# Stacking two of the four batches the other way round, so that the 64x64 score products address all four quadrants of TensorE

## The chip, the core and the metric

The kernel runs on one core of one Trainium2 chip. The metric is the device time of one execution in microseconds (us), and less is better. Three executions of the kernel before took 624.39 to 625.46 us, with a median of 624.98 us.

## The reference

Two layers follow each other, in float32. The first is a linear recurrence over time (RWKV time mixing) for 4 batches, 8 heads, 768 tokens and 48 channels per head:

```python
for t in range(S):
    cur = einsum('bhd,bhe->bhde', u[None] * k[t], v[t])
    y[t] = einsum('bhd,bhde->bhe', r[t], state + cur)
    state = w[None, :, :, None] * state + einsum('bhd,bhe->bhde', k[t], v[t])
```

Its output, 3072 tokens of 384 features, goes into a gated feed-forward network with a root-mean-square norm ahead of it:

```python
xn = x / sqrt(mean(x * x, axis=-1) + 1e-06) * rms_g
g = xn @ w_gate
out = (g * sigmoid(g) * (xn @ w_val)) @ w_out      # 384 -> 1536 -> 384
```

## The kernel before

**Time mixing in chunks.** The 768 tokens are cut into 12 chunks of 64 (`NS`, `L`). Within a chunk the recurrence becomes matrix products: scores between the chunk's keys and receptances, weighted by powers of the decay `w`, times the values, plus the state from before the chunk. `mixing(s)` adds the operations of chunk `s` to a plan. The names of its steps, which the text uses, are these:

- R: `decay_r` multiplies r by the decay powers `up`, on DVE, into the tile `ME`. Rc: `copy_r` copies the odd heads' partitions 64 to 127 into `MO`, on ACT. K: `decay_k` multiplies k by `down` in place, on DVE.
- A: `products` forms the scores on TensorE. Of the 8 heads, the even ones lie on partitions 0 to 47 and the odd ones on partitions 64 to 111 (side `z`). There are 4 batches, 4 pairs of heads and 2 sides, so 32 products of 48x64 by 48x64. Even heads use rows 0 to 63 of the array and write PSUM partitions 64 to 127; odd heads use rows 64 to 127 and write partitions 0 to 63. Two batches (one `half`) fill one bank (`at`), and the two halves are done one after the other.
- d: `diagonal` puts the bonus for the current token on the diagonal of the scores' tile, on ACT, from `du`, which DVE computes with three passes over `TOK` (`bonus_1` to `bonus_3`, the second with the table `utab`). m: `masked` copies the scores below the diagonal over it, on DVE.
- Y: `outputs` multiplies `ME` and `MO` (half scores, half decayed r) with `VS` (half values, half state), 32 products of 128x64 by 128x64 on TensorE. The two sides write different halves of the PSUM partitions.
- h and U: `state_k` weights the keys with the table `wk`, and `states` forms the new state, on TensorE. `keep_states` copies it back.
- After Y, `keep_squares`, `keep_outputs` and a norm (`scaled` on DVE) give `xa`, and `exchange` copies it with its partition halves swapped into `xb`.

Chunk 0 (`quick`, `early`) is done differently: A goes half by half, the diagonal comes from an extra product E of `ku`, and the weighted keys come from a product T (`turn_k`).

**Feed-forward.** Chunks 0 and 1 go through plain gate, value and output products (`gate_val`, `add_cell`), while the weights arrive from memory in pieces. Each piece is loaded by SP, split by ACT (`ulp`) and DVE (`bits`) and joined by GpSimd (POOL). Later chunks are taken two at a time through a seven-product scheme (`group`, `second_layer`). A product of this kind is 6 matmuls of 64x128 by 64x256.

**What sets the order.** `Plan.add` takes each operation with its engine, an assumed cost, and the names that it reads and writes. `Plan.schedule` lays them out by assumed start times and due times. `Plan.search` tries 4 times 2000 random changes of those due times for the operations of the first chunks. `Plan.give` then issues everything in the order of the planned starts. So each engine's order is fixed when the kernel is built, and waits between engines are semaphores. The plan prices A at 2.0 us. `warm` fills idle stretches of TensorE in the first 27 us of the plan with products of `ones`. One of these is two records in the trace.

**How the trace shows a matmul.** Every float32 matmul of the program stands in the trace as two LDWEIGHTS and two MATMUL records. The 32 products of one A are therefore 64 MATMUL records.

Of the kernel before, what the change touches and what calls it, by code (L numbers as in the profile page):

```python
# [41 lines left out]
FP32 = mybir.dt.float32  # L42
# [8 lines left out]
P = 128  # L51
# [10 lines left out]
B, H, S, D = 4, 8, 768, 48  # L62
HP = H // 2
L = 64
# [175 lines left out]
def fast(ctx, tc, chan, tok, vpad, wka, wkb, wot, cols, u_row, out, bad):  # L240
# [23 lines left out]
    def c_tile(shape, name, dtype=FP32):  # L264
        return const.tile(shape, dtype, name=name)
# [4 lines left out]
    wraw, ucol, gcol = col[:, 0:HP], col[:, HP : 2 * HP], col[:, 2 * HP :]  # L270
    utab = c_tile([P, HP, D], "utab")
    eps = c_tile([P, 1], "eps")
# [17 lines left out]

    ident = c_tile([P, P], "ident")
    make_identity(nc, ident)
# [24 lines left out]
    gdup = rows_out[:, 0].rearrange("p j f -> p (j f)")[:, 0 : HP * 2 * L].rearrange("p (h z t) -> p h z t", h=HP, z=2)  # L317
    wk = c_tile([P, HP, D], "wk")
    pows = {1: wcol}
# [18 lines left out]
    def keep_token_powers(bank):  # L338
        ps = bank.rearrange("p (h c) -> p h c", h=HP)
        act.copy(wk[64:128], ps[64:128, :, 0:D])  # L340
        act.copy(wk[0:64], ps[0:64, :, 64 : 64 + D])

    def state_decay(z, p):

        rows = slice(64 * z, 64 * z + D)
        act.mul(
            KH[rows, z, :, p, :], free_dims(ident[rows, 64 * z : 64 * z + D], (0, B), (1, D)), pows[L][rows, p : p + 1]
        )

    def w_range():  # L350
# [20 lines left out]
    def load_u():  # L371
        for z in range(2):
            src = bass.AP(tensor=u_row.tensor, offset=u_row.offset + z * HP * D, ap=[[0, 64], [1, HP * D]])
            sp.dma_start(out=utab[64 - 64 * z : 128 - 64 * z].rearrange("p h d -> p (h d)"), in_=src)

# [53 lines left out]

    def decay_r(s, lo=0, hi=B):  # L430

        dve.tensor_mul(ME[:, lo:hi], CH[:, 0, lo:hi], free_dims(up, (0, hi - lo), (L, HP), (1, L)))

    def copy_r(s, lo=0, hi=B):
        act.copy(MO[64:128, lo:hi], ME[64:128, lo:hi])

    def decay_k(s, lo=0, hi=B):
        dve.tensor_mul(CH[:, 1, lo:hi], CH[:, 1, lo:hi], free_dims(down, (0, hi - lo), (L, HP), (1, L)))

    def bonus_1(s):  # L440
        dve.tensor_mul(TOK[:, 0], TOK[:, 0], TOK[:, 1])

    def bonus_2(s):
        dve.tensor_mul(TOK[:, 0], TOK[:, 0], free_dims(utab, (0, B), (D, HP), (1, D)))

# [26 lines left out]
    def state_k(s, z):  # L472

        rows = slice(64 - 64 * z, 128 - 64 * z)
        dve.tensor_mul(KH[rows, z], TOK[rows, 1], free_dims(wk[rows], (0, B), (D, HP), (1, D)))

    def turn_k(bank, half):

        pk = bank[:, 0 : 2 * HP * D].rearrange("p (b h d) -> p b h d", b=2, h=HP)
        for bl in range(2):  # L480
            b = 2 * half + bl
            for p in range(HP):
                for z in range(2):
                    rows = slice(64 * z, 64 * z + D)
                    pe.matmul(
                        pk[64 - 64 * z : 128 - 64 * z, bl, p, :], CH[rows, 1, b, p, :], KH[rows, z, b, p, :], start=True,
                        stop=True, skip_group_check=True,
                    )
# [5 lines left out]

    def products(bank, half, ks, even, odd):

        pa = bank.rearrange("p (b h t) -> p b h t", b=2, h=HP)
        for bl in range(2):
            b = 2 * half + bl
            for p in range(HP):  # L500
                for rows, to, m in ((slice(0, D), slice(64, 128), even), (slice(64, 64 + D), slice(0, 64), odd)):
                    pe.matmul(
                        pa[to, bl, p, :], ks[rows, b, p, :], m[rows, b, p, :], start=True, stop=True,
                        skip_group_check=True,
                    )

# [9 lines left out]
    def outputs(bank, half):  # L516

        py = bank.rearrange("p (i t) -> p i t", i=HP)
        for bl in range(2):
            b = 2 * half + bl  # L520
            for p in range(HP):
                for z, m in ((0, ME), (1, MO)):
                    pe.matmul(
                        py[64 * z : 64 * z + 64, p, bl * L : (bl + 1) * L], VS[:, z, b, p * L : (p + 1) * L],
                        m[:, b, p, :], start=True, stop=True, skip_group_check=True,
                    )
# [219 lines left out]
    def mixing(s):  # L746
# [3 lines left out]
        if early:  # L750
            t = "ac"[s]
            add("ACT", 1.6, ["w", "CHk0", "CHk1"], ["ku"], lambda: u_k(s, ku), name=f"ku {s}")
            for half in range(2):
                add(
                    "PE", 1.05, ["ku", "CHr0", "CHr1"], [f"{t}{half}"],
                    lambda half=half: products(bank_of[t][:, half], half, ku, CH[:, 0], CH[:, 0]), name=f"E {s}",
                    rows=True,
                )
        else:
            add("DVE", 0.95, ["TOKk"], ["TOKr"], lambda: bonus_1(s), port=True, name=f"bonus1 {s}")  # L760
            add("DVE", 0.95, ["utab"], ["TOKr"], lambda: bonus_2(s), port=True, name=f"bonus2 {s}")
            add("DVE", 0.94, ["TOKr"], ["du"], lambda: bonus_3(s), name=f"bonus3 {s}")
        for part in ((0, 2), (2, 4)) if early else ((0, 4),):
            hs = range(part[0] // 2, part[1] // 2)
            n = len(hs)
            keys = lambda *names: [f"{x}{h}" for x in names for h in hs]
            add(
                "DVE", 0.12 + 0.55 * n, ["up"] + keys("CHr"), keys("MEr", "MEt"),
                lambda part=part: decay_r(s, *part), port=True, name=f"R {s}",
            )  # L770
            add("ACT", 0.16 + 0.44 * n, keys("MEt"), keys("MOr"), lambda part=part: copy_r(s, *part), name=f"Rc {s}")
            add(
                "DVE", 0.12 + 0.55 * n, ["down"], keys("CHk"), lambda part=part: decay_k(s, *part), port=True,
                name=f"K {s}",
            )
        two = [next_at() for _ in range(2)]

        def scores(half):
            products(two[half][0], half, CH[:, 1], ME, MO)

        score_keys = [[f"CHk{half}", f"MEr{half}", f"MOr{half}"] for half in range(2)]
        if quick:
            for half in range(2):
                add("PE", 1.05, score_keys[half], [two[half][1]], lambda half=half: scores(half), name=f"A {s}", rows=True)
        else:
            add(
                "PE", 2.0, score_keys[0] + score_keys[1], [two[0][1], two[1][1]], lambda: [scores(0), scores(1)],
                name=f"A {s}", rows=True,
            )
# [82 lines left out]
        else:  # L872
# [11 lines left out]
            else:  # L884
# [8 lines left out]
                add("DVE", 0.35, ["ms'"], ["ms"], lambda: refine(ms[:, 0], ms[:, 1]), name=f"inv {s}")  # L893
            add("DVE", 0.4, ["ms"], ["diag"], lambda: on_diagonal(ms[:, 0], diag), port=True, name=f"diag {s}")
            add("PE", 0.45, ["diag"], [key], lambda bank=bank: spread(bank, diag), name=f"spread {s}")
# [5 lines left out]
        if not turned:  # L901
# [3 lines left out]
        add(  # L905
            "PE", 1.58, ["KH0", "KH1", "VSv", "VSs0", "VSs1"] + [f"khd{z}{i}" for z in range(2) for i in range(HP)],
            [last[0][1], last[1][1]], lambda: [states(last[half][0], half) for half in range(2)], name=f"U {s}",
# [9 lines left out]
    add("DVE", 0.43, ["pw"], ["down"], lambda: dve.tensor_mul(down, pw_rev, by_inv), port=True, name="down")  # L917
    add("DVE", 0.22, [], ["dmask"], lambda: dve.tensor_add(dmask, ident[:, 0:64], ident[:, 64:128]), port=True)
    for z in range(2):
        for i in range(HP):  # L920
            add("ACT", 0.34, ["pw"], [f"khd{z}{i}"], lambda z=z, i=i: state_decay(z, i), name="khd")

    def token_tables():
        add(
            "DVE", 0.86, ["pw"], ["r0", "r1"], lambda: [
                dve.tensor_mul(gdup[:, :, z, :], pw_rev, free_dims(pows[L // 2], (1, HP), (0, L))) for z in range(2)
            ], port=True, name="gdup",
        )
        bank, key = next_at()
        add("PE", 0.9, ["r0", "r1"], [key], lambda bank=bank: token_powers(bank), name="wk")  # L930
        add("ACT", 0.7, [key], ["wk"], lambda bank=bank: keep_token_powers(bank), name="wk")

# [76 lines left out]
    add("DVE", 0.4, ["w"], ["count"], w_range)  # L1009
    add("DVE", 0.0, ["rounded", "up", "down", "wk", "dmask", "ku"], ["sums"], begin_sums)  # L1010
    for n, reads, writes in (
# [679 lines left out]
```

## Time and profile before

| what | value |
|---|---|
| median of three executions | 624.98 us (624.39 to 625.46) |
| profiled execution: span from first to last instruction | 622.6 us |
| median less that span | 2.4 us |
| mean granted TensorE clock in the profiled execution | 0.994 |
| busy, share of the span: PE | 607.1 us, 98% |
| PEld (weight loads) | 537.7 us, 86% |
| DVE | 443.0 us, 71% |
| ACT | 355.7 us, 57% |
| POOL | 42.7 us, 7% |
| busy in 150 to 550 us: PE, DVE, ACT | 399.5, 286.0 and 237.0 of 400 us |

The page lists no time of the profiled execution other than its span; what lies around the span is taken as the 2.4 us between it and the median. In the page and in the queries, a group of instructions carries the tiles that it writes and reads: `at<-ME,chan` and `at<-MO,chan` are A's even and odd heads, `at<-ME,VS` and `at<-MO,VS` are Y, and `at<-VS,KH` is U. All lines are L92, a helper that records every operation, so groups are told apart by their tiles. Busy time on PE counts overlapping matmuls once. A wait is named after the instruction that released it.

### The profile page before, as it was taken

What the parts mean: (1) busy time and instruction counts of PE and PEld (TensorE: products, weight loads), DVE (VectorE), ACT (ScalarE), POOL (GpSimd) and SP (SyncE); (2) the same over time, 40 slices, a digit from 0 to 9 for tenths busy, and PEclk for the clock granted to TensorE, in tenths of its full rate; (3) what the DMA queues carried; (4) which work ended last, traced back from release to release, by engine and by line L of the source; (5) the groups of instructions that cost most, each with busy time, mean ns of one, the idle gap of its engine ahead of it and who ended that gap; (6) DMA issues with size and microseconds to landing.
All of it is one profiled execution on the core that took longest, in us unless ns stands there. A gap on an engine that the chain in (4) does not pass through costs nothing.

```text
span 622.6 us, 15324 instructions
## 1 busy us (share of the span) xinstructions
PE 607.1 (98%) x6536; PEld 537.7 (86%) x6536; DVE 443.0 (71%) x621; ACT 355.7 (57%) x906; POOL 42.7 (7%) x41
## 2 busy tenths in 40 slices
PE   8989999999999999999999999999999999999994
PEld 8867877776888899888899888899888899988994
DVE  7789878888875797657997557897556886455631
ACT  6896958356577434844978354887444784232200
POOL 2144134200000000000000000000000000000000
PEclk9899999999999999999999999999999999999998
DMA  8596673013730123235141424141324211310001
GB/s 284 173 330 222 212 246 106 2 58 77 232 106 2 35 76 100 81 101 178 33 134 29 127 63 147 55 144 43 97 82 113 99 36 29 80 52 2 1 14 44
DMA packets 22782, 62.92 MB, mean 101 GB/s; under 512 B 3152, under 2 KB 10160, under 8 KB 21296
## 3 DMA queue, kind: packets, MB, share of 16 engines
q1 hardware_dynamic: 22112, 61.46, 32.0%
q8 instruction: 53, 0.87, 0.6%
q10 hardware_dynamic: 592, 0.39, 0.2%
q14 instruction: 25, 0.20, 0.1%
HBM read 55.94 MB, written 4.72 MB: 97 GB/s over the span
## 4 chain that ended last, share of the span: by engine, by line
PE 90%; DVE 3%; ACT 2%; issue 2%; DMA 1%; POOL 0%; POOLq 0%; ACTq 0%
PE bank_b L92 30%; PE bank_a L92 26%; PE bank_c L92 23%; PE at L92 11%; DMA TOK<-in_tok_dram 1%; DVE bits L92 1%; ACT ME L92 1%; ACT MO L92 1%; DVE TOK L92 1%; DVE rows_out L92 1%; DMA yT<-last_heads 0%; DVE xa L92 0%; DVE chan L92 0%; DVE ME L92 0%; POOL wa L92 0%
## 5 line engine op out<-in xcount | busy, mean ns | idle before, releaser
L92 DVE TENSOR_TENSOR gv<-bank_b,m 128x512 f32<-128x512 f32 x90 | 62.2, 691 | 70.7 <-PE bank_b L92 70.2
L92 ACT ACTIVATE gv<-gv 128x512 f32<-128x512 f32 (+1 forms) x60 | 31.3, 523 | 50.9 <-DVE gv L92 50.6
L92 PE MATMUL bank_b<-xa,wa 64*128 64x256 f32 x444 | 55.3, 382 | 0.5 <-DVE gv L92 0.5
L92 DVE TENSOR_TENSOR gv<-bank_c,gv 128x512 f32<-128x512 f32 x60 | 41.5, 692 | 17.8 <-PE bank_c L92 16.9
L92 PE MATMUL bank_a<-wo,h 128*128 128x192 f32 (+1 forms) x264 | 50.4, 344 | 0.0
L92 ACT ACTIVATE gv<-bank_a 128x256 f32<-128x256 f32 x30 | 11.5, 383 | 67.0 <-PE bank_a L92 66.9
L92 ACT ACTIVATE ME<-dmask,du 64x64 f32<-64x64 f32 x176 | 46.1, 331 | 6.1 <-DVE du L92 5.4
L92 PE MATMUL bank_a<-xa,wa 64*128 64x256 f32 x396 | 49.4, 382 | 0.0
L92 PE MATMUL bank_a<-xb,wb 64*128 64x256 f32 x396 | 48.6, 378 | 0.0
L92 PEld LDWEIGHTS bank_b<-xa,wa 64*128 64x128 f32 x444 | 41.9, 187 | 6.8 <-issue 1.0
L92 ACT ACTIVATE MO<-dmask,du 64x64 f32<-64x64 f32 x176 | 46.5, 336 | 1.1 <-DVE du L92 0.6
L92 PEld LDWEIGHTS bank_a<-wo,h 128*128 128x128 f32 x264 | 43.4, 190 | 3.6 <-issue 0.3
L92 PE MATMUL bank_b<-t,wb 64*128 64x256 f32 x360 | 44.1, 377 | 0.0
L92 PE MATMUL bank_c<-t,s 64*128 64x256 f32 x360 | 44.0, 377 | 0.0
L92 PE MATMUL bank_b<-t,s 64*128 64x256 f32 x360 | 43.9, 376 | 0.0
L92 PE MATMUL bank_c<-xb,s 64*128 64x256 f32 x360 | 43.9, 376 | 0.0
L92 ACT ACTIVATE rows_out<-rows_out 128x384 f32<-128x384 f32 x72 | 40.0, 557 | 5.9 <-DMA rows_out<-in_wka_dram 4.6
L92 PEld LDWEIGHTS bank_a<-xa,wa 64*128 64x128 f32 x396 | 37.4, 187 | 6.8 <-issue 2.5
L92 PEld LDWEIGHTS bank_a<-xb,wb 64*128 64x128 f32 x396 | 38.1, 187 | 4.5
L92 PEld LDWEIGHTS bank_c<-t,s 64*128 64x128 f32 x360 | 34.7, 187 | 4.5 <-issue 0.5
L92 PEld LDWEIGHTS bank_b<-t,s 64*128 64x128 f32 x360 | 34.9, 187 | 4.0
L92 PEld LDWEIGHTS bank_c<-xb,s 64*128 64x128 f32 x360 | 34.9, 187 | 4.0
(152 smaller groups left out, 1247.2 us busy)
## 6 DMA issues: line engine op xcount, KB each, us to landing
chan<-in_chan_dram SPq DMA_DIRECT2D x11, 1024.0 KB, 6.0
TOK<-in_tok_dram SPq DMA_DIRECT2D x11, 768.0 KB, 4.9
VS<-in_vpad_dram SPq DMA_DIRECT2D x24, 256.0 KB, 4.2
raw<-in_wot_dram SPq DMA_DIRECT2D x8, 576.0 KB, 5.2
rows_out<-in_wka_dram SPq DMA_DIRECT2D x12, 384.0 KB, 3.5
rows_out<-in_wkb_dram SPq DMA_DIRECT2D x12, 384.0 KB, 3.3
rows_out<-in_wot_dram SPq DMA_DIRECT2D x12, 384.0 KB, 3.5
out_dram<-rows_out SPq DMA_DIRECT2D x43, 96.0 KB, 2.3
```

The source lines that it names most:

```text
L92: return lambda *args, **kwargs: self.tc.keep_in_program_order(give(*args, **kwargs))
```

## The change

Batches 2 and 3 are stored with the two sides of the partition halves exchanged wherever tokens lie on partitions (`TOK`, `VS`, `KH`, the scores in `ME` and `MO`). For them the even heads' scores go to PSUM partitions 0 to 63 and the odd heads' to 64 to 127. In A the products of half 0 and half 1 are issued alternately, two of each, and every half keeps its own bank, so four consecutive products address four different 64x64 quadrants of the array. The plan's price of A goes from 2.0 to 1.05.

R is issued half by half. Half 1 of the decayed r stays where A reads it, in place in `chan` (for chunk 0 in `sq`), and two copies bring it to the partitions of `MO` and `ME` where Y needs it. The tables `utab` and `wk` get a second stacking. The constant decay blocks in `KH` are made for two batches and copied across for the other two. `ident` moves to a pool that is freed when the loading stage ends. Nothing changes in the number of products.

```diff
-    utab = c_tile([P, HP, D], "utab")
+    utab = c_tile([P, 2, HP, D], "utab")
...
-    ident = c_tile([P, P], "ident")
+    ident = raws.tile([P, P], FP32, name="ident")
...
     def keep_token_powers(bank):
         ps = bank.rearrange("p (h c) -> p h c", h=HP)
-        act.copy(wk[64:128], ps[64:128, :, 0:D])
-        act.copy(wk[0:64], ps[0:64, :, 64 : 64 + D])
+        for e in range(2):
+            rows = slice(64 - 64 * e, 128 - 64 * e)
+            for x in range(2):
+                z = e ^ x
+                act.copy(wk[rows, x], ps[rows, :, 64 * z : 64 * z + D])
...
-            KH[rows, z, :, p, :], free_dims(ident[rows, 64 * z : 64 * z + D], (0, B), (1, D)), pows[L][rows, p : p + 1]
-        )
+            KH[rows, z, 0:2, p, :], free_dims(ident[rows, 64 * z : 64 * z + D], (0, 2), (1, D)), pows[L][rows, p : p + 1]
+        )
+
+    def crossed_decay(e):
+
+        act.copy(KH[64 * e : 64 * e + D, e, 2:4], KH[64 - 64 * e : 64 - 64 * e + D, 1 - e, 0:2])
...
-        for z in range(2):
-            src = bass.AP(tensor=u_row.tensor, offset=u_row.offset + z * HP * D, ap=[[0, 64], [1, HP * D]])
-            sp.dma_start(out=utab[64 - 64 * z : 128 - 64 * z].rearrange("p h d -> p (h d)"), in_=src)
+        for h in range(2):
+            src = bass.AP(tensor=u_row.tensor, offset=u_row.offset + h * 2 * HP * D, ap=[[0, 64], [1, 2 * HP * D]])
+            sp.dma_start(out=utab[64 * h : 64 * h + 64].rearrange("p x h d -> p (x h d)"), in_=src)
...
-    def decay_r(s, lo=0, hi=B):
-
-        dve.tensor_mul(ME[:, lo:hi], CH[:, 0, lo:hi], free_dims(up, (0, hi - lo), (L, HP), (1, L)))
-
-    def copy_r(s, lo=0, hi=B):
-        act.copy(MO[64:128, lo:hi], ME[64:128, lo:hi])
+    def crossed_r(s):
+
+        if s:
+            return CH[:, 0, 2:4]
+        return sq.rearrange("p h t -> p (h t)")[:, 0 : 2 * HP * L].rearrange("p (b h t) -> p b h t", b=2, h=HP)
+
+    def decay_r(s, half):
+        to = crossed_r(s) if half else ME[:, 0:2]
+        dve.tensor_mul(to, CH[:, 0, 2 * half : 2 * half + 2], free_dims(up, (0, 2), (L, HP), (1, L)))
+
+    def copy_r(s, e):
+
+        act.copy((MO, ME)[e][64 - 64 * e : 128 - 64 * e, 2:4], crossed_r(s)[64 * e : 64 * e + 64])
+
+    def side_r(s):
+        act.copy(MO[64:128, 0:2], ME[64:128, 0:2])
...
-    def products(bank, half, ks, even, odd):
-
-        pa = bank.rearrange("p (b h t) -> p b h t", b=2, h=HP)
+    def products(banks, halves, ks, moving):
+
         for bl in range(2):
-            b = 2 * half + bl
             for p in range(HP):
-                for rows, to, m in ((slice(0, D), slice(64, 128), even), (slice(64, 64 + D), slice(0, 64), odd)):
-                    pe.matmul(
-                        pa[to, bl, p, :], ks[rows, b, p, :], m[rows, b, p, :], start=True, stop=True,
-                        skip_group_check=True,
-                    )
+                for half in halves:
+                    pa = banks[half].rearrange("p (b h t) -> p b h t", b=2, h=HP)
+                    for z in range(2):
+                        rows, e = slice(64 * z, 64 * z + D), z ^ half
+                        pe.matmul(
+                            pa[64 - 64 * e : 128 - 64 * e, bl, p, :], ks[rows, 2 * half + bl, p, :],
+                            moving(half, z)[rows, bl, p, :], start=True, stop=True, skip_group_check=True,
+                        )
...
             add(
-                "PE", 2.0, score_keys[0] + score_keys[1], [two[0][1], two[1][1]], lambda: [scores(0), scores(1)],
+                "PE", 1.05, score_keys[0] + score_keys[1], [two[0][1], two[1][1]], lambda: scores([0, 1]),
                 name=f"A {s}", rows=True,
             )
```

`turn_k`, `outputs`, `bonus_2` and `state_k` address the same number of elements by the new stacking. The arrays that the host lays out (`tok`, `vpad`, `u_row`) follow it.

## The prediction

> **What bounds the kernel now.** I read the busy line and the slices of the page first, then the shares of the chain that ended last.
>
> ```profile
> PE 607.1 (98%) x6536; PEld 537.7 (86%) x6536; DVE 443.0 (71%) x621; ACT 355.7 (57%) x906; POOL 42.7 (7%) x41
> PE   8989999999999999999999999999999999999994
> PE 90%; DVE 3%; ACT 2%; issue 2%; DMA 1%; POOL 0%; POOLq 0%; ACTq 0%
> ```
>
> TensorE is full in all slices but the first few and the last, and 90% of the chain is TensorE. So time taken off TensorE between about 40 and 613 us shortens the whole, unless another engine makes it wait. Next I read the chain in order of time around the last chunk's mixing (start, duration, what):
>
> ```profile
> 498.31 1.57 PE at L92 x64
> 499.88 3.45 PE bank_a L92 x20
> 503.33 2.01 PE at L92 x64
> 505.34 4.75 PE bank_a L92 x28
> 510.09 2.02 PE at L92 x64
> 512.11 3.93 PE bank_b L92 x23
> ```
>
> By the timeline these three `at` pieces are U (of the chunk before), A and Y, with output products packed between them. A holds TensorE for 2.01 us and nothing waits. The timeline shows how A spends it (start, duration, then the instruction):
>
> ```profile
> 503.37 0.22 PE L92 MATMUL at<-ME,chan 48*64 48x64 f32 x1
> 503.37 0.14 PEld L92 LDWEIGHTS at<-ME,chan 48*64 48x64 f32 x1
> 503.37 0.22 PE L92 MATMUL at<-MO,chan 48*64 48x64 f32 x1
> 503.38 0.14 PEld L92 LDWEIGHTS at<-MO,chan 48*64 48x64 f32 x1
> 503.43 0.22 PE L92 MATMUL at<-ME,chan 48*64 48x64 f32 x1
> ```
>
> The two sides start together, with weight loads between them, and the next pair follows 0.058 us later (32 starts between 503.26 and 505.12 us: the first step 0.10, the others 0.058). A is thus 32 periods of two quadrants: 32 x 0.058 = 1.86, plus about 0.15 at entry and exit, gives the 2.01 seen. Two quadrants are idle.
>
> The first 40 us are another stage. Their chain has waits in it:
>
> ```profile
> 30.88 4.89 issue
> ...
> 35.80 0.42 POOL wb L92
> 36.23 1.36 issue
> 37.59 1.01 POOL wa L92
> ```
>
> There TensorE waits for weight pieces being converted and for the masks of chunk 1 (its one long wait for `DVE ME` is 2.3 us).
>
> **What the Trainium skill says.** "TensorEngine Tiling (Array Packing)", section Tiling Modes, gives four independent 64x64 tiles. The trace shows two kinds of pair sharing the array: A's two use different rows, Y's two share all 128 rows and differ in columns, and both step at 0.058 us. All four at once no row of before shows. "TensorE: Matmul & The Clock Gate", Part 3, says that a weight load overlaps a running matmul only when the row groups differ. Y contradicts it here: its two LDWEIGHTS, on the same rows, start 0.006 us apart within the same 0.058. The same part reports row and column packing composing (10.6 times for 16 tiles); no run here shows that yet. "TensorEngine Tiling", Restrictions and Gotchas, forbids different row tiles in one PSUM bank at a time. A of before has its two row tiles in one bank, on different partitions, without a visible wait. In the changed A the tiles that share partitions write different banks, as the two sides of the gate products do already.
>
> **The change part by part.**
>
> *A.* Four quadrants per period make 16 periods. Per array row the demand equals Y's (two weight loads, two moving streams), and per array column it equals the gate products' (two row tiles, two banks). I take 0.060 us a period: 0.96, plus 0.15, gives 1.11, against 2.01: 0.90 saved. Bounds: at best 16 x 0.058 + 0.1 = 1.03 (0.98 saved). At worst the quadrants don't overlap: 2.01, nothing saved. Between them lies a limit by instructions. The fastest steady rate in the trace is U's, 8 records (4 loads, 4 matmuls) per 0.090 us, 0.011 each; A's 128 records at that rate take 1.44 + 0.15 = 1.59 (0.42 saved). Against that limit: within a period records start 0.002 to 0.006 us apart, so eight would need some 0.03 of 0.058 us.
>
> *Where it counts.* There are 11 such A's (chunks 1 to 11); chunk 0 goes half by half and keeps its price. Those at 58, 88, 159, 216, 289, 312, 384, 408, 480 and 503 us have TensorE work right behind them: 10 x 0.90 = **9.0 us**. The one at 30 us ends in the long wait above, so I count nothing for it: what is late next is Y of chunk 1, held by masks on DVE.
>
> *R and its copies.* The rows:
>
> ```profile
> L92 ACT COPY MO<-ME 64x1024 f32<-64x1024 f32 x11 | 11.5, 1042 | 1.8 <-DVE ME L92 1.6
> L92 ACT COPY MO<-ME 64x512 f32<-64x512 f32 x2 | 1.2, 616 | 0.0
> L92 DVE TENSOR_TENSOR ME<-chan,up 128x1024 f32<-128x1024 f32 x11 | 13.4, 1219 | 2.7 <-DMA chan<-in_chan_dram 2.5 <-PE at L92 0.3
> L92 DVE TENSOR_TENSOR ME<-chan,up 128x512 f32<-128x512 f32 x2 | 1.4, 688 | 1.2 <-DMA chan<-in_chan_dram 1.2
> ```
>
> Per chunk ACT pays 3 x 0.62 - 1.04 = +0.81, DVE 2 x 0.69 - 1.22 = +0.16; over 11 chunks 8.9 and 1.7 us. From 150 to 550 us ACT is busy 59% and DVE 71%, so I cost both at nothing. The cover is thinnest just ahead of Y: in the last mixing ACT runs diagonals without a break from 501.8 to 508.2, the last mask ends at 509.26 and Y starts at 510.02, a margin of 0.76 us. The new copies need only R, which is done before A, so they can stand ahead of the diagonals. A no longer waits for the half 1 copies, only Y does. They also read `chan`, so the next chunk's `chan` load (1024 KB, 6.0 us to landing) waits for them on SP's queue, and the loads behind it with it. They come before Y, and a chunk's A's lie 20 to 70 us apart, so that stays covered.
>
> *Re-addressed and constant work.* `bonus_2` and `state_k` keep 768 elements (0.95 to 0.99 us). `wk` has two copies more (2 x 0.31), `crossed_decay` is two of 48x384 (0.47 each, as `VS<-at`), and `state_decay` gets half as long. That is some 1 us of ACT in the first 30 us. `utab`'s two loads double from 48 KB on SP's queue.
>
> *The first 40 us replanned.* The order of the program built from the changed kernel shows more than the diff. The first 384 KB weight piece now stands before the two `chan` loads on SP. From 512 KB landing in 4.1 us and 1024 KB in 6.0, that is about 1.4 us for all that follows. On ACT eight diagonals (2.1 us) stand before the root of chunk 0 where the 1.04 us copy stood: 1.1 us more. So `xa` of chunk 0 ends near 25.2 + 2.5 = 27.7 us. The first gate product stood at 28.0, waiting for a weight piece that is now converted earlier, so it starts about as before. Behind it four gate products (5.2 us) now come ahead of chunk 1's Y, which before stalled 2.5 us and then 0.7; on DVE two 576-wide conversions (1.7 to 2.7 us each) now come ahead of its masks. I take the sum as zero, between -2.5 (the stalls go) and +3 (start and masks late, nothing covered). On PE, the order from 150 us on is nearly that of before.
>
> Sum: span 622.6 - 9.0 = 613.6. With the 2.4 us between the span and the median of the runs shown, **616.0 us**.
>
> **The rivals.**
>
> *Issue-limited A.* At U's rate, 10 x 0.42 = 4.2 saved: 620.8. For it: A's period is 0.058 at 64 columns and U's 0.045 at 48, which is 0.0008 per column and 0.005 that doesn't scale; that part may be paid per record. Against it: the bursts.
>
> *The start eats part.* A is as fast as I say, the first 40 us lose 3: 619.0.
>
> *Slower: quadrants sharing rows take turns.* If the weight load of a quadrant waits for the matmul on the same rows, A stays at 2.01, while the plan has placed masks, Y and the next work as if it took 1.05. The masks come 0.95 us later than planned; with the 0.81 us of copies on ACT against a margin of 0.76, Y waits up to 1.0 us in each of 11 mixings. Half of that gives 624.98 + 5.5 = 630.5. It decides once A takes more than about 1.9 us. Y's loads on shared rows speak against it.
>
> *No effect.* A unchanged, delays absorbed: 625.
>
> **How the numbers follow.** Forecast as worked out 0.72 (616.0, own range 613 to 618.5), start eats part 0.06, issue-limited 0.12, slower 0.07, no effect 0.03. About 0.2%, 1.25 us, is what a measurement of this kernel can tell from no change. The first three are faster: 0.90. The range takes in A at 1.03 with the start 2.5 better (10 x 0.98 + 2.5 gives 612.7) and the issue-limited case: 612.7 to 620.8.
>
> **What would show it.** A's 64 matmul records in about 1.0 us, four starting within 0.03 us, period near 0.06; the next TensorE piece 1.1 us after A's start; TensorE still at 9 in all slices from 40 to 600 us; `gv`, `wo` and Y rows unchanged in length. Wrong: a period near 0.12 (turns) or 0.09 (issue); waits of PE for `DVE ME` or `ACT ME` in many chunks (copies late); the first `bank_a<-third` product, at 144.9 us before, coming later than 143.5 (the start lost).

## The result, and the profile after

Eight executions of the changed kernel took 619.86 to 623.71 us, median **621.48 us**. Eight of the kernel before, on the same chip, took 623.95 to 627.50, median 624.87. The ratio is 0.9949, with a 95% interval of 0.9931 to 0.9968: faster, by 3.4 us where 9.0 were forecast. The profiled execution's span is 619.3 us, 3.3 less than before.

The busy line, TensorE's slices and the shares of the chain, from the page of the changed kernel:

```profile
PE 602.3 (97%) x6552; PEld 528.7 (85%) x6552; DVE 443.0 (72%) x632; ACT 365.6 (59%) x933; POOL 43.5 (7%) x41
PE   7989999999999999999999999999999999999994
PE 92%; DVE 3%; issue 2%; ACT 1%; POOL 0%; ACTq 0%; POOLq 0%; DVEq 0%
```

ACT has the added 9.9 us (8.9 for R's copies and about 1 for constants were priced); DVE has none, where 1.7 were priced. TensorE is busy 4.8 us less, but the span is only 3.3 us shorter, so it stands idle 1.5 us longer than before. The slices, 15.5 us each, are too coarse to show where.

The chain of the changed kernel in order of time around the last chunk's mixing (start, duration, what):

```profile
493.08 1.57 PE at L92 x64
494.65 1.50 PE bank_b L92 x12
496.15 1.29 PE bank_c L92 x12
497.44 3.45 PE bank_a L92 x20
500.89 1.09 PE at L92 x64
501.98 4.75 PE bank_a L92 x28
```

The second `at` piece is A: 64 records in 1.09 us, where it was 2.01. The timeline of the same place shows why (start, duration, instruction):

```profile
500.93 0.22 PE L92 MATMUL at<-ME,chan 48*64 48x64 f32 x1
500.93 0.22 PE L92 MATMUL at<-MO,chan 48*64 48x64 f32 x1
500.94 0.23 PE L92 MATMUL at<-chan 48*64 48x64 f32 x2
500.98 0.22 PE L92 MATMUL at<-ME,chan 48*64 48x64 f32 x1
```

`at<-chan` are the products of half 1, whose decayed r stays in `chan`. Four products start within 0.01 us, and the next four follow at the old period. All eleven A's look like this: 11 x 0.92 = 10.1 us went out of TensorE's work. The span has only 3.3 of them, so 6.8 us were lost again elsewhere.

Two marks in the trace say where. The first is the first `bank_a<-third` product, which opens the stretch after the weights are in. The second is the start of TensorE's last product. The marks come from one profiled execution of each kernel, the medians from four to eleven executions, and each ratio is to the runs of before in the same comparison (medians 624.87 to 625.82 us). The rows below *after* are the experiments of the next section.

| kernel | median, us (range) | ratio to before (95%) | first third product | from there to the last product |
|---|---|---|---|---|
| before | 624.87 (623.95 to 627.50) | | 144.92 | 470.26 |
| after | 621.48 (619.86 to 623.71) | 0.9949 (0.9931 to 0.9968) | 144.63 | 467.18 |
| one_half_at_a_time | 630.49 (628.16 to 632.86) | 1.0075 (1.0046 to 1.0105) | 148.62 | 473.16 |
| before_order | 619.11 (618.04 to 619.78) | 0.9893 (0.9873 to 0.9913) | 147.64 | 463.01 |
| du_first | 619.37 (616.10 to 622.35) | 0.9897 (0.9866 to 0.9927) | 148.70 | 464.20 |
| piece_back | 621.87 (620.76 to 622.50) | 0.9941 (0.9921 to 0.9961) | 144.39 | 467.18 |
| du_late_in_before | 633.88 (632.54 to 638.32) | 1.0141 (1.0116 to 1.0167) | 145.79 | 477.91 |
| du_late_again | 628.80 (628.36 to 629.46) | 1.0058 (1.0045 to 1.0071) | 145.08 | 474.15 |
| two_orders | 617.90 (617.74 to 619.59) | 0.9881 (0.9864 to 0.9897) | 144.71 | 464.10 |
| no_fill | 618.44 (616.61 to 619.15) | 0.9885 (0.9871 to 0.9900) | 143.20 | 464.09 |
| root_first | 618.45 (616.94 to 618.79) | 0.9884 (0.9869 to 0.9898) | 143.61 | 464.10 |
| few_fillers_only | 620.15 (619.47 to 621.41) | 0.9920 (0.9908 to 0.9932) | 143.05 | 467.19 |
| few_fillers | 616.97 (616.43 to 617.57) | 0.9864 (0.9850 to 0.9878) | 143.90 | 464.09 |

Three A's lie before the first mark and eight behind it. They should have brought 2.8 and 7.4 us; they brought 0.3 and 3.1. So there are two losses, **2.5 us at the start and 4.3 us later**. The late stretch repeats well: the three traces with the late order of after and the fast A (after, piece_back, few_fillers_only) give 467.18 or 467.19 us. The first mark does not: two kernels with the same order up to it have it at 144.63 (after) and 148.70 (du_first). The three with before's order up to it lie at 144.92 to 145.79 (before, du_late_again, du_late_in_before).

Nearly all of the later one sits in two places, one in each of two like cycles. Here is the chain of the changed kernel at the first of them, ahead of the feed-forward group of chunks 6 and 7:

```profile
329.44 7.81 PE bank_c L92 x48
...
337.28 1.02 DVE rows_out L92 x2
338.30 0.86 DVE t L92
339.17 0.88 DVE du L92
...
340.13 1.05 ACT ME L92 x4
...
341.20 0.59 ACT m L92
...
341.82 0.70 DVE gv L92
...
342.57 1.57 PE bank_b L92 x12
```

From 337.28 to 342.57 the end is set by DVE and ACT, not by TensorE: the output sums (`rows_out`), a sum `t` for the next group, `du` of chunk 8, a diagonal on ACT that needs `du`, the copy to `m`, `gv`, and only then the product. The DVE timeline of the changed kernel adds how long DVE stood idle ahead of this (the bracket is the wait and what ended it):

```profile
333.05 0.95 DVE L92 TENSOR_TENSOR xa<-xb,xa 128x768 f32<-128x768 f32 x1
337.28 1.02 DVE L92 TENSOR_TENSOR rows_out<-bank_c,rows_out 128x384 f32<-128x384 f32 x2 [3.28 <-PE bank_c L92]
338.22 0.95 DVE L92 TENSOR_TENSOR t<-xb,t 128x768 f32<-128x768 f32 x1
339.08 0.95 DVE L92 TENSOR_REDUCE du<-TOK 128x16 f32<-128x768 f32 x1
339.95 0.55 DVE L92 TENSOR_TENSOR rows_out<-bank_c,rows_out 128x384 f32<-128x384 f32 x1
341.82 0.69 DVE L92 TENSOR_TENSOR gv<-bank_b,m 128x512 f32<-128x512 f32 x1 [0.73 <-ACT m L92]
```

P5 and P3 are the kernel's names for two of the seven products of the second layer; each is 12 matmuls, so 24 records. The two sums at 337.28 read the half of `bank_c` that P5 filled, with the first 24 of the 48 records above. But they start when P3, the other 24, has ended; whether the wait can be had for P5 alone wasn't tried. In the kernel before these sums wait for `bank_c` too, but there `du` stands ahead of them:

```profile
328.23 0.95 DVE L92 TENSOR_REDUCE du<-TOK 128x16 f32<-128x768 f32 x1
341.17 1.02 DVE L92 TENSOR_TENSOR rows_out<-bank_c,rows_out 128x384 f32<-128x384 f32 x2 [2.67 <-PE bank_c L92]
```

The new plan, which lets those sums start at P5's end, put `du` and the second half of R behind them. So ACT waits for `du` (16.0 us in two waits of 8.0 in the view of waits), and TensorE waits first for the bank that the last of these sums frees and then for `gv`:

```profile
340.55 1.57 PE L92 MATMUL bank_c<-t,s 64*128 64x256 f32 x12 [0.52 <-DVE rows_out L92]
342.57 0.70 PE L92 MATMUL bank_b<-xa,wa 64*128 64x256 f32 x4 [0.45 <-DVE gv L92]
```

The bracket counts from the modelled end of the matmul before. Counted from its start, at 339.66 and 341.74, less the usual step of 0.22 us, the waits are 0.68 and 0.61 us; later waits of TensorE are given in this way. The second cycle repeats both, 96 us later. The four make 2.6 of the 4.3 us; short waits of about 0.1 us behind each pair add about 1.

### The profile page after: what moved, and what is told of

Read it like the earlier page. It is cut to its first block, busy times and chain, and to the rows that moved or that the text cites. A ratio compares the mean times of both kernels' runs of the same rounds, so it can differ in the third digit from the quotient of the medians.

```text
span 619.3 us, 15403 instructions
## 1 busy us (share of the span) xinstructions
PE 602.3 (97%) x6552; PEld 528.7 (85%) x6552; DVE 443.0 (72%) x632; ACT 365.6 (59%) x933; POOL 43.5 (7%) x41
## 4 chain that ended last, share of the span: by engine, by line
PE 92%; DVE 3%; issue 2%; ACT 1%; POOL 0%; ACTq 0%; POOLq 0%; DVEq 0%
PE bank_b L92 31%; PE bank_a L92 27%; PE bank_c L92 24%; PE at L92 10%; DVE bits L92 1%; DVE rows_out L92 1%; DVE ms L92 0%; DVE chan L92 0%; DVE gv L92 0%; ACT ME L92 0%; DVE du L92 0%; DVE t L92 0%; ACT m L92 0%; POOL wb L92 0%; DVE sq L92 0%
```

## The experiments

All but one_half_at_a_time change only the order in which `Plan.give` issues the operations, and the fillers (the products of `ones` that `warm` adds): the search is replaced by a list of planned starts, in which some are changed.

```diff
-    goals = p.search(cells, goals, free, n_searched, n_first, 2000)
-    p.give(p.schedule(goals, free, len(p.ops), n_first), warm)
+    planned = [
...
+    ]
+    p.give(planned, warm)
```

**one_half_at_a_time.** The changed kernel, all else kept, with A's halves one after the other:

```diff
-                "PE", 1.05, score_keys[0] + score_keys[1], [two[0][1], two[1][1]], lambda: scores([0, 1]),
+                "PE", 1.05, score_keys[0] + score_keys[1], [two[0][1], two[1][1]], lambda: [scores([half]) for half in range(2)],
```

> The changed kernel in its own order, with the two halves of A issued one after the other again, so that two quadrants work at a time; stacking, copies and tables as changed. Theory 1 (A's gain reaches the end where TensorE is full): A goes back from 1.09 to 2.01 us in 11 chunks; 8 to 10 us more than the changed kernel, 629 to 632 us. Theory 2 (the shorter A only moves waits, and the chains on DVE and ACT set the pace): under 4 us more, 622 to 625 us.

Measured 630.49 us, slower than before. A takes 1.84 us, not the 2.01 that was expected, and the late stretch is 5.98 us longer than after: 8 x 0.75. So issuing the halves in turn brings 0.75 of the 0.92 us; quadrants and banks alternate together here and were not tried apart. The other 0.17 us is in the trace too: around the seam between the halves three periods hold four products each, for instance two of half 0 and two of half 1 between 510.79 and 510.81 us. Products of half 1 (`at<-chan`) start there ahead of the last ones of half 0, though the kernel issues all of half 0 first.

This run also shows that the late loss doesn't come from the shorter A. Eight A's at 1.84 should have brought 1.4 us against before, and the stretch is 2.9 longer: 4.3 us are lost again, with the same four waits of 0.68 and 0.61 us. The total is that of the prediction's slower rival, 630.5, which stood for an A that stays at 2.01. But the first mark, at 148.62, is 4.0 us later than after, of which the three slower A's explain at most 2.3, so the agreement is partly chance.

**before_order.** The changed kernel's instructions in the order of the kernel before:

```diff
-    starts of the changed kernel's plan
+    starts of the plan of before; two halves of R where R stood, three copies where one stood
```

> All instructions of the changed kernel, issued in the planned order of the kernel before: the two parts of R where R stood, the three copies where the one copy stood, everything else at its old place. Theory 1 (the order ate the gain: the plan was made anew and the new order is worse for reasons that the plan doesn't see): A takes 1.09 us in each of 11 places, 10 of which have TensorE work right behind them, so the span falls by about 10 x 0.92 = 9.2 from 622.6, to 613.5, and the time to 615 to 617 us. Theory 2 (the added work ate it: 0.81 us of ACT and 0.16 of DVE per chunk, the larger tables at the start): the time stays at 620 to 622 us, with TensorE waiting for ACT ahead of Y.

Measured 619.11. The late stretch is 463.01, 7.25 less than before, against 7.36 from eight A's: the whole late gain is there, with all added copies on ACT. So behind the first mark the copies cost nothing, and the loss is one of order. The chain at the same place has no engine but TensorE in it:

```profile
332.49 7.80 PE bank_c L92 x48
340.29 1.50 PE bank_a L92 x12
341.79 1.29 PE bank_b L92 x12
```

The start, on the other hand, is 3.0 us later than after (147.64). The old order suits it badly: TensorE waits 1.7 us inside A of chunk 1, where the trace names ACT's copies to `wk` (four now, where two were) that free the bank of half 1, and 1.1 inside U of chunk 1. Here, then, added copies do cost time.

**du_first.** The changed kernel's order, with two DVE instructions moved in each of the two cycles:

```diff
-    t3, u4, c22, t4, bonus_3, c12, second half of R
+    t3, bonus_3, second half of R, u4, c22, t4, c12
```

(`t3` and `t4` are sums for the next group, `u4`, `c22` and `c12` the output sums; `bonus_3` makes `du`.)

> The changed kernel in its own order, with four DVE instructions moved: in the mixings of chunks 8 and 10 the reduction to du and the second half of R go ahead of the sums that wait for the last product of the second layer, instead of behind them. Theory 1 (TensorE waits at the first group after the second layer, at 339.7, 341.7, 435.5 and 437.6 us, because these stand in DVE's queue ahead of what frees its banks): the four waits of 0.6 to 0.7 us go, and some of the 0.4 us of short waits behind each pair; 2.6 to 4.2 us less, 617.3 to 619 us. Theory 2 (ACT and DVE simply have too much to do there with the added copies): the waits come back elsewhere, 621 us or a little less.

The late stretch is 464.20, 2.98 less than after; both waits are gone in both cycles. A wait of 0.91 at 205 us is new, but it is no cost of the move: up to 338 us the order is that of after, and DVE waited there 2.33 us for the landing of `TOK` where it waited 1.38 in after. Without it the move would have won 3.9. The median, 619.37, is blurred by starts that differ (616.10 to 622.35 us); in the profiled execution, one of the longest, the first mark came 4 us late.

**du_late_in_before and du_late_again.** The reverse, in the kernel before, A at 2.01 us as ever: only `bonus_3` of chunks 8 and 10 goes behind the sums, and with it their diagonals on ACT.

```diff
-    bonus_3, ..., u4, c22, t4, c12
+    ..., u4, c22, t4, bonus_3, c12
```

> The kernel before, with its own order everywhere but in the mixings of chunks 8 and 10: there du is computed on DVE behind the sums that wait for the last output product (as the changed kernel has it), and on ACT one diagonal stands ahead of the copy to m1 and seven behind it. Nothing else differs, A is still 2.01 us. Theory (this order alone costs the late part of the gain): two waits of TensorE near 0.9 us and some short ones appear at the first group products of both cycles, 1.5 to 2.1 us a cycle, so 3 to 4.2 us more than before: about 628 to 629 us. Rival (the late loss comes from the shorter A or from the copies of R added on ACT, whatever the order): no change, 625 us.

Measured 633.88, more than either theory. The two pairs of waits appear, but also one of 2.2 us in each cycle, at 352.4 and 451.8: I had put all seven diagonals ahead of a silu of the group, and the changed kernel puts two behind it. du_late_again corrects that:

> As du_late_in_before (the kernel before, du of chunks 8 and 10 behind the sums on DVE), but with ACT's diagonals placed as in the changed kernel: one ahead of the copy to m1, five behind it, and the last two behind the first silu instead of all seven ahead of it. Theory (the 2.2 us waits at 352.4 and 451.8 us of du_late_in_before came from the diagonals ahead of that silu, the 0.68 and 0.61 us waits from du behind the sums): the two long waits go, the two pairs of short ones stay, 3 to 4.2 us above before: 629 to 630 us. Rival (du late costs the long wait too, by the masks or the buffers behind it): still 633 to 634 us.

Measured 628.80. The long waits are gone; the stretch is 3.89 us longer than before. The waits of TensorE, from the timeline of du_late_again, are those of the changed kernel:

```profile
344.68 1.57 PE L92 MATMUL bank_c<-t,s 64*128 64x256 f32 x12 [0.52 <-DVE rows_out L92]
346.69 1.13 PE L92 MATMUL bank_b<-xa,wa 64*128 64x256 f32 x8 [0.45 <-DVE gv L92]
```

The place of `du` and, with it, of its diagonals on ACT costs 3.9 us in the kernel before, with nothing else of the change. Taken back in the changed kernel it wins as much, so it accounts for 3.9 of the 4.3 us. The other 0.4 lies among smaller waits that differ between the two orders (one of 0.33 at 180 us is new in the changed kernel, one of 0.66 at 249 us is in before alone), and was not tried apart.

**piece_back.** The changed order, with the first weight piece's load, split and conversions back behind chunk 0's work:

```diff
-    SP: load 2, chan; ACT: ulp 2 first; DVE: bits 2, powers
+    SP: chan, ..., load 1, load 2; ACT: ulp 1, ulp 2; DVE: powers, ..., bits 1, bits 2
```

> The changed kernel in its own order, with one weight piece (load, its ACT part, its two DVE parts) moved from ahead of everything to its old place behind chunk 0's work. Theory 1 (the start is late because DVE waits for this piece to land before it computes the decay powers: the first R stands at 8.2 instead of 6.4 us): the first R is back at 6.4, chunk 0's outputs come 1.8 us earlier, and 1 to 2 us of it reach the end, 619.5 to 620.5 us. Theory 2 (what comes after, ACT's diagonals and the conversion of the last piece of the first quarter at 42 us, holds TensorE anyway): first R earlier, but the first product of the paired scheme still at about 144.6 us, 621 us.

Measured 621.87, no different from after, and the first mark moves by 0.24 us. That this piece is the loss at the start falls. In the changed kernel's trace the piece does delay DVE: its conversion heads DVE's queue, waits 2.81 us for the landing, and `powers` starts at 5.00 instead of 2.42. But most of it is absorbed behind, as the next runs show. What goes with the piece is an unsteady start: with it first, three profiled executions had the first product of E at 7.72, 9.04 and 10.01 us; without it six lie between 6.95 and 7.62.

**two_orders.** piece_back's order for the first 150 us, the order of before for the rest:

```diff
-    starts of piece_back
+    starts of piece_back below 150 us, those of before_order from there on
```

> The changed kernel with the first 150 us of its own order, but the first weight piece loaded behind the work of chunk 0, and with the order of the kernel before from 150 us on. Theory (start and late part are two separate losses): the first third product at 144.4 us as with the piece moved back, and from there to the end 463.0 as with the order of before: last product at 607.4, 4.2 less than with the piece moved back; about 617 us. Rival (what an earlier start wins, the later order gives back at the seam): first third product or the stretch behind it 2 us longer, about 619 us, no better than the order of before alone.

Measured 617.90, with both marks near the expected ones; 1.0 us stays at the seam, in a wait at 153 us. The two losses are separate.

**no_fill, root_first, few_fillers_only, few_fillers.** These four change the start. few_fillers_only stands on piece_back, the others on two_orders. The fillers between T and Y of chunk 0 are left out, and in two of them most of the later ones:

```diff
-        if until < 27:
-            for _ in range(int((until - since - 0.3) / (0.22 if since else 0.5))):
+        if until < 27 and not 14 < since < 15:
+            for _ in range(min(int((until - since - 0.3) / (0.22 if since else 0.5)), 4 if since else 15)):
```

no_fill and root_first have the first line alone, the other two both. root_first and few_fillers also have, on ACT:

```diff
-    diagonal 1, diagonal 1, root of chunk 0; ..., four diagonals, two copies of R, ulp 5
+    root of chunk 0, diagonal 1, diagonal 1; ..., ulp 5, four diagonals, two copies of R
```

> As two_orders, without the 8 filler products of ones (16 records) between T and Y of chunk 0. They stood from 15.4 to 17.9 us behind the stall in T, at half the granted clock, while the masks that Y needs were done at 15.2. Theory (the fillers hold the start): Y of chunk 0 at about 15.6 instead of 18.1. The root of chunk 0 then waits on ACT for two diagonals of chunk 1 whose du is done at 18.0, so only 0.5 to 1.5 us reach the state product of chunk 0: about 616 us. Rival (the fillers keep the granted clock up; without them Y itself runs at half clock for longer): Y takes over 3 us, no change or 1 us more, 617 to 618 us.

Y of chunk 0 came at 14.81 us, but took 3.02 us up to the next product, most of it at half clock (2.01 in the kernel before), and the 32 filler records further on took 5.28. The first mark is 1.5 us earlier, the median no better than two_orders. Both theories were half right.

> As no_fill, and on ACT the root of chunk 0 ahead of the last two diagonals of chunk 1, and the split of weight piece 5 ahead of four other diagonals of chunk 1. Theory (ACT's queue sets the rest of the first 45 us): the state product of chunk 0 starts 2 us earlier, and the 2.3 us wait of TensorE near 39.5 us for the joined piece 5 shrinks below 1: 2 to 4 us less than no_fill, about 613 us. Rival (masks and Y of chunk 1, or the joining of pieces on POOL, become late instead): the same waits stand a few us further on, and the time is that of no_fill.

The wait for weight piece 5 is gone, but the state product of chunk 0 comes later: the diagonal of the norm was done at 26.2, and 32 filler records, most of them at half clock, held the spread (the product that reads this diagonal) until 29.16. The time is that of no_fill.

> The changed kernel with the first weight piece moved back (as piece_back), without the 8 fillers between T and Y of chunk 0 and with 4 instead of 16 between the norm's squares and the spread of chunk 0; every other instruction in its place. Theory (the fillers lie on the path of chunk 0, but weight piece 5 is split late on ACT whatever TensorE does): the state product of chunk 0 starts 1.5 to 2.5 us earlier, the wait for piece 5 near 39.5 us grows by nearly as much, the first third product stays within 0.5 us of 144.4: 621 to 622 us. Rival (the fillers alone held the start): it comes 1.5 to 2.5 us earlier, 619.5 to 620 us.

The first mark came 1.34 us earlier, at 143.05, and the time is 620.15: the rival is nearer, though it missed too. The wait for piece 5 did not grow; it shrank from 2.33 to 1.13, since ACT's queue came earlier as well.

> As root_first (the late order of before, root of chunk 0 and split of piece 5 early, no fillers between T and Y), and with 4 instead of 16 fillers between the squares and the spread of chunk 0. In root_first the diagonal of the norm was done at 26.2 us and the spread started at 29.2, behind 32 filler records at half clock. Theory (these fillers hold chunk 0 once the root is early): spread at about 26.4, first third product at 141 to 142 instead of 143.6: about 616 us. Rival (with fewer fillers the clock is granted at half for longer, and the products of chunk 0 pay for it): first third product at 143.6 or later, 618.4 us or more.

The spread came at 26.85, near the expected 26.4, but the first mark at 143.90, as the rival had it: U of chunk 0 took 2.52 us instead of 1.83. The windows of this kernel show the clock (window, its length, then busy time and records of PE, PEld, DVE, ACT and POOL, then the granted clock, DMA share and GB/s):

```profile
20.00:22.00 2.00, 1.51 (x7) 1.51 (x8) 0.16 (x1) 2.00 (x7) 0.78 (x1) 0.63 0.15 51
22.00:25.00 3.00, 3.00 (x15) 3.00 (x16) 2.88 (x5) 0.90 (x5) 0.99 (x1) 0.50 0.42 88
25.00:30.00 5.00, 4.99 (x60) 4.07 (x62) 3.81 (x9) 4.91 (x14) 2.01 (x2) 0.50 0.94 339
```

After a gap of 2.4 us at 18.1 to 20.5 TensorE runs at half clock until 30. Still, at 616.97 this kernel has the lowest median of the study, 8.1 us under before in its own comparison, and its interval lies wholly under that of the changed kernel. Against two_orders the intervals overlap, so what the fillers bring is not settled.

## Why the prediction was right or wrong

**A: right.** 1.11 us was forecast and 1.09 measured. The period stayed at 0.058, now for four quadrants, so the issue limit and the taking of turns both fall. What "TensorEngine Tiling (Array Packing)", section Tiling Modes, of the Trainium skill says of four independent 64x64 tiles holds here.

**The copies at nothing: right behind the first mark.** before_order has them all, and keeps 7.25 of 7.36 us there. The place that I took for the thinnest, ahead of Y, shows no wait of TensorE for `DVE ME` or `ACT ME` in the changed kernel. Between 20 and 42 us ACT was busy without a break, and there they delay what stands behind them, as the start below shows.

**"On PE, the order from 150 us on is nearly that of before": true, and the step that failed.** I compared TensorE's order there and took the other engines' to follow. On DVE the plan had moved `du` and half of R behind sums whose wait it does not know of. The order of DVE and ACT was counted as nothing and is 4.3 us, 3.9 of them by the place of `du`. That DVE is busy 71% and ACT 59% from 150 to 550 us said nothing about this one place. A line of the view of waits of before could have warned (the total in us, how often, the longest):

```profile
DVE rows_out L92 <- PE bank_c L92: 15.5, 8, 3.5
```

Whatever is put behind such a wait on DVE comes late.

**The start as zero: mis-sized, inside its ends.** My sum had two A's (1.8 us) counted ahead of the first mark and zero for the rest; 0.3 came, so the start cost 1.5 us. The parts:

- The load ahead of `chan` was priced at 1.4 us. E came 1.30 late and A of chunk 0 1.80. I didn't see that the piece's conversion stands at the head of DVE's queue.
- The root on ACT came at 25.23 instead of 21.47, and `xa` of chunk 0 ended at 29.70, where I had 27.7. The first gate product, said to start "about as before" at 28.0, came at 30.62.
- Four windows of the changed kernel, in the columns given above, hold a part that I had not thought of:

```profile
14.00:16.00 2.00, 0.49 (x6) 0.44 (x6) 1.94 (x3) 0.47 (x2) 0.00 (x0) 1.00 1.01 393
16.00:18.00 2.00, 2.00 (x16) 2.00 (x15) 1.93 (x4) 1.97 (x5) 0.00 (x0) 0.77 0.97 297
18.00:20.00 2.00, 2.00 (x34) 1.77 (x35) 1.97 (x3) 0.27 (x1) 0.00 (x0) 0.50 0.93 381
20.00:22.00 2.00, 2.00 (x42) 1.74 (x38) 0.59 (x2) 1.65 (x6) 1.00 (x1) 0.88 0.76 304
```

  TensorE started nothing inside T from 13.72 to 15.51; later, at 17.1, the granted clock fell to 0.5, until 20.5. Fillers and Y of chunk 0 ran in that stretch: Y took 2.84 us from its first start to its last, where it took 1.86 before. The kernel before has a stretch of the same length at 0.50, from 21.7 to 25.1 us, but there it fell on fillers and the two records of the spread:

```profile
20.00:22.00 2.00, 2.00 (x18) 1.93 (x17) 2.00 (x3) 1.57 (x4) 0.00 (x0) 0.93 0.21 60
22.00:25.00 3.00, 2.74 (x11) 2.29 (x11) 2.45 (x6) 2.42 (x7) 0.00 (x0) 0.50 0.02 5
```

- The stalls at Y of chunk 1 (2.5 and 0.7) went, as forecast. New is a wait of 2.33 us at 39.70 for weight piece 5: ACT, busy without a break from 20.35 us with diagonals, the new copies and `wk`, splits it only at 40.57. root_first removed this wait and won nothing by it; there fillers, most of them at half clock, held the work ahead.

How the 2.5 us divide among root, fillers, clock and piece 5 stays open: each was moved, and another took its place.

**The range.** "A is as fast as I say, the start loses 3" was given 619.0; a late loss of an order's making was among no rival. With it, 9.2 - 4.3 - 1.5 is 3.4 us. That this is the measured gain is no second proof, since both losses are read from the same trace. The sign that I named, the first third product later than 143.5, was there (144.63), but it told only of the smaller loss.

## What to carry to other kernels

When a change alters the costs that a planner works with, compare the order on every engine, not only on the one that bounds: an instruction of no weight that slips behind a waiting one on an in-order engine holds everything that needs it. Look for the long waits of engines off the path first; they are harmless only as long as nothing urgent stands behind them. And test the order apart from the change: issued in the old order, the new work showed at once that its late gain was whole.

## What the runs showed of the hardware

- Four products that pairwise share array rows or columns kept the period of two: 64 records start within 0.94 us, where 1.86 were needed. In one_half_at_a_time products of half 1 also started ahead of products of half 0 that the kernel issues earlier.
- "TensorE: Matmul & The Clock Gate", Part 1, of the Trainium skill has the clock halved after an idle window of about 3.4 us and full again after as long under load. The traces here do not fit it: in the changed kernel 0.50 came after a gap of 1.8 us, in root_first none followed within 5 us of a gap of 2.3 us, in the kernel before it came at 21.7 us with no idle time of TensorE over 0.16 us since 14.2, and in few_fillers 0.50 lasted for 8 us in which TensorE was busy for 7.99. The measurement decides: the length of one gap does not tell when the clock falls, and the recovery can take longer. What does decide stays open.
- TensorE stood still for 1.1 to 2.3 us behind its 222nd MATMUL record in eleven of the thirteen traces, whatever that record was (a filler or part of T), and went on between 14.2 and 15.6 us. In the two traces that reached it only at 17.8 and 19.0 us there was no gap. No instruction in the trace ends it. But in each of the eleven the first 16 KB packet of the queue that the profile's page calls `q8 instruction` landed 1.4 to 1.6 us before TensorE went on (at 13.99 against 15.51 in the changed kernel), and in the two without a gap it had landed 2.4 and 2.6 us before the 222nd record. So TensorE seems to have waited for its next instructions; no run tested that.
